# Packing V into 16-bit parts: the element operations go from VectorE to GpSimd, in two-operand instructions

## The chip, the cores and the metric

The kernel runs on one core of a Trainium2 chip. The metric is device time in microseconds for one execution. Before the change it is 1028.72 us, the median of three runs (1028.23 to 1029.83).

## What is computed

The reference mixes two branches over the same x (2048 rows of 512), with a gate of its own for each row:

```
g = sigmoid((x * gate_w).sum(-1))
q = x @ wq          # 32 heads of 16
k = x @ wk          # one head of 16, shared by all
v = x @ wv
a = softmax(q k^T / 4) v, heads joined, @ wo
b = silu(x @ w1) @ w2        # 512 -> 1792 -> 512
out = g * a + (1 - g) * b
```

All inputs and the output are fp32. The kernel keeps nearly fp32 exactness by splitting operands into two fp16 parts and adding three products, and, for the softmax's values, by "packing" V.

## The kernel before, in words

**Attention.** There are 16 rounds, one for each pair of a chunk of 512 query rows (c) and a group of 8 heads (o). A round has 32 steps; a step takes 64 keys. A step has two score units on TensorE (`scores`, L1186: 8 matmuls into a PSUM tile S), two exponentials on ScalarE (`exponential`, L1192, 128x1024 each, into a P buffer) and the product with V (`pv`, L1223). That product is made in one of two ways:

- in fp32 with V itself (the tile VF), whole (called W here) or in two halves of 256 columns (h);
- with the packed V (the tile VP, fp16): first a pass over the upper 16 bits of P (called A), then a pass over the remainder (called B). The remainder L = P - upper(P) is made by VectorE in two instructions of 128x1024 (`low`, L1198; its buffers are the L tiles, later the two raw tiles and freed parts of xs).

`decide` (L1400) lets a step take the packed way only if V's rows for that step are already packed: `k >= packed[0]` means W or h. Besides, VectorE must have room for the two remainders (`low_next`, L1411). So until the packing of the first 16 steps' keys is done, all steps take the fp32 way.

**The packing.** `v_parts` (L372) packs one half of V (16 of the 32 blocks of 64 keys) in five parts, all on VectorE: a maximum and a power of two per block (`first`), rounding to a high part `hi` and a rest `lo` (`first`, `second`), a sum of rest terms (`second`), then a chain of digit roundings (`third`, `fourth`), and two instructions that write VP (`fifth`). Its wide instructions have 128x256 elements, its small ones 128x16. The scratch tiles are U and T2 (T in the profile). `pack` (L1297) and `pack_next` hand the ten parts one after the other to VectorE's list of tasks.

**Other work.** TensorE also runs the feed-forward and the projections as a stream of passes (`Stream`, L1053; line 832; called F here), 8 matmuls to a pass when two outputs run side by side. Weights arrive in pieces: `Pieces.load` (L172) issues a DMA into one of two raw tiles, VectorE splits it in two instructions (L207, L208), and then the next DMA into that tile is issued **from GpSimd's queue** (L190). The cast of the hidden layer is also a DMA from GpSimd's queue (H<-e, L898). Otherwise GpSimd is idle after the start.

**The order.** Inside `attention` the order on every engine is written by a small planner: it holds a time for TensorE, ScalarE and VectorE (`now`), takes the engine whose next piece of work is ready first (`advance`, L1604) and emits it. Work for VectorE is put on a list by `task(due, ready, length, f)`, and the earliest due that is ready goes next (`dve_next`, L1539). Engines then run their instructions strictly in the order emitted, and wait on semaphores. The planner keeps no time for GpSimd.

Of the kernel before, what the change touches and what calls it, by code (L numbers as in the profile page):

```python
# [31 lines left out]
CAST, LEAD, ENDS = 3.0, 3, 2  # L32

# [20 lines left out]
def kernel(  # L54
# [317 lines left out]
    def v_parts(tiles, half):  # L372
# [5 lines left out]
        u, m, h, w = (ab[:, :, n:n + 1] for n in range(4))  # L378
        to = lambda t: t.to_broadcast([128, NKT, 16])
        nu, inv = (nus[:, n:n + 1].to_broadcast([128, NKT, 16]) for n in (0, 2))  # L380
        tt = lambda out, a, b, op: nc.vector.tensor_tensor(out, a, b, op=op)
        ts = lambda out, a, k: nc.vector.tensor_scalar(out, a, k, None, op0=OP.mult)
        stt = lambda out, a, k, b: nc.vector.scalar_tensor_tensor(out, a, k, b, op0=OP.mult, op1=OP.add)

        def first():
# [3 lines left out]
            ts(u, u, 2.0 ** -10)  # L389
# [3 lines left out]
            tt(hi, hi, to(m), OP.add)  # L393

        def second():
            tt(hi, hi, to(m), OP.subtract)
            tt(lo, V, hi, OP.subtract)
            tt(s, lo, nu, OP.mult)
            nc.vector.tensor_reduce(w, s, axis=AX.X, op=OP.add)

        def third():
            for a in MAGIC * 4.0 ** -DIG, -MAGIC * 4.0 ** -DIG, 0.5 * 4.0 ** -DIG:
                stt(w, u, a, w)
            tt(un, to(u), nu, OP.mult)
            stt(s, un, -0.5, to(w))
            stt(s, un, MAGIC, s)

        def fourth():
            stt(s, un, -MAGIC, s)
            tt(k[:, :, 1:15], s[:, :, 1:15], s[:, :, 0:14], OP.subtract)  # L410
            tt(k[:, :, 0:1], s[:, :, 0:1], s[:, :, 15:16], OP.subtract)
            nc.vector.tensor_copy(k[:, :, 15:16], s[:, :, 15:16])
            tt(k, k, inv, OP.mult)

        def fifth():
            tt(VP[:, these, 1:17], hi, k, OP.add)
            tt(VP[:, these, 17:32], lo[:, :, 0:15], k[:, :, 0:15], OP.subtract)

        return first, second, third, fourth, fifth


# [369 lines left out]
    def attention(ctx, scale_of, t_scale, shifts, split_pieces, chores, q_todo, early, gates_):  # L791
# [437 lines left out]
        def begin():  # L1229
# [22 lines left out]
            for a in range(2):  # L1252
# [7 lines left out]
                def copies(t, a=a, v4=v4):  # L1260
# [7 lines left out]
                    else:  # L1268
# [3 lines left out]
                        pack_next(pack(), t)  # L1272
# [24 lines left out]
        def pack():  # L1297
            t2 = wp.tile([128, 32, 32], F32, name="T2").rearrange("p a b -> p (a b)")
            tiles = [wp.tile([128, 512], F32, name="U"), t2[:, 0:512], t2[:, 512:1024]]
            for half in range(2):  # L1300
                for n, f in enumerate(v_parts(tiles, half)):
                    yield 1.7, f, (half + (n == 4)) * NKT

        def pack_next(gen, t):
            x = next(gen, None)
            if x:
                length, f, upto = x

                def run(t):
                    f()  # L1310
                    packed[0] = upto
                    pack_next(gen, t)

                task(t + 4, t, length, run)
# [74 lines left out]
        n_early, n_begin = [3 * KD * len(early)], [0]  # L1389
        packed, n_mm, n_exp, head = [0], [0], [0], [0]  # L1390
# [214 lines left out]

# [94 lines left out]
```

## Time and profile before

| | |
|---|---|
| median of three runs | 1028.72 us |
| span of the profiled execution | 1033.2 us |
| PE (TensorE) busy | 1012.3 us, 98% |
| ACT (ScalarE) busy | 993.1 us, 96% |
| DVE (VectorE) busy | 916.4 us, 89% |
| POOL (GpSimd) busy | 62.7 us, 6% |
| first exponential starts | 28.23 us |
| last TensorE instruction starts | 1024.22 us |

The profiled execution is known by its span; it lies 4.5 us above the median of the runs. Rows of a timeline give start, duration, engine, line, operation, output tile, input tiles and the number of instructions merged. Rows of groups give the count, the busy time in us and the mean in ns of one, and then the idle time of the engine before them. A busy PE is modelled, so a unit of TensorE work is priced here by the distance of its start from the next unit's start.

### The profile page before, as it was taken

Reading aid. Unit: us, or ns where it says so; the run is one execution under the profiler, and the core shown is the slowest. Engines: PE = TensorE matmul, PEld = TensorE weight load, DVE = VectorE, ACT = ScalarE, POOL = GpSimd, SP = SyncE. Lnnn points to the kernel's source line nnn. Section 1 sums busy time; section 2 is a strip of 40 time slices with the busy share of each in tenths; the row PEclk is TensorE's granted clock in tenths of the full one; section 3 lists DMA queues with packets and bytes.
Section 4 is the critical chain, followed back from the end, with each engine's and each line's share of the span. In section 5 each row is a group of like instructions: output and inputs, shape, how many; then the busy total and the mean of one; then the engine's idle time right before and its main releaser. Section 6 shows DMA issues by size and latency. Waiting matters only on the chain.

```text
span 1033.2 us, 69440 instructions
## 1 busy us (share of the span) xinstructions
PE 1012.3 (98%) x32605; PEld 615.0 (60%) x32605; DVE 916.4 (89%) x1191; ACT 993.1 (96%) x1109; POOL 62.7 (6%) x141
## 2 busy tenths in 40 slices
PE   8999999999999999999999999999999999999996
PEld 7345655565656666656566665566665565565563
DVE  7778887889899999999989899798999889989994
ACT  5899999999999999999999999999999999999994
POOL 5001111100000000000000000000000000000000
PEclk9999999999999999999999999999999999999999
DMA  5122322221011111100101110110111110100001
GB/s 207 53 76 65 93 58 61 70 62 19 15 19 41 39 36 30 20 20 15 35 16 35 50 30 20 30 25 10 34 32 25 33 48 10 35 10 14 10 4 47
DMA packets 28114, 40.12 MB, mean 39 GB/s; under 512 B 5689, under 2 KB 19370, under 8 KB 27818
## 3 DMA queue, kind: packets, MB, share of 16 engines
q0 software_dynamic: 10656, 15.73, 7.3%
q1 hardware_dynamic: 16442, 19.27, 5.9%
q8 instruction: 257, 4.21, 1.7%
q10 hardware_dynamic: 720, 0.59, 0.2%
q14 instruction: 39, 0.32, 0.1%
HBM read 19.98 MB, written 8.25 MB: 27 GB/s over the span
## 4 chain that ended last, share of the span: by engine, by line
PE 71%; issue 19%; ACT 6%; DVE 1%; DMA 1%; POOL 1%; SPq 0%; ACTq 0%; POOLq 0%; DVEq 0%
PE pm L832 26%; PE pv L1223 24%; PE S L1186 17%; ACT P L1192 4%; ACT xs L1192 1%; PE pm L836 1%; DMA xn<-in_A_x_dram 1%; PE pt L336 1%; POOL H L898 1%; PE pv L1211 1%; DMA H<-e 0%; ACT e L886 0%; DVE L L1198 0%; PE S L1179 0%; DVE e L889 0%
## 5 line engine op out<-in xcount | busy, mean ns | idle before, releaser
L1192 ACT ACTIVATE P<-S 128x1024 f32<-128x1024 f32 x764 | 731.4, 1081 | 11.8 <-PE S L1186 7.8
L1186 PE MATMUL S<-qb,KT 50*32 50x512 f16 x8096 | 471.6, 379 | 3.3 <-ACT P L1192 1.7
L1186 PEld LDWEIGHTS <-KT 50*32 50x32 f16 x8096 | 203.3, 90 | 186.6 <-issue 96.7
L1198 DVE TENSOR_TENSOR L<-P 128x1024 f16<-128x1024 f32 x242 | 288.8, 1216 | 20.0 <-ACT P L1192 16.7
L832 PE MATMUL pm<-xs,w1s 64*32 64x512 f16 x5376 | 274.9, 375 | 2.4 <-DVE e L889 1.7
L832 PE MATMUL pm<-w2s,H 64*32 64x512 f16 x5376 | 267.9, 375 | 2.0 <-DVE e L889 1.2
L1192 ACT ACTIVATE xs<-S 128x1024 f32<-128x1024 f32 x260 | 256.8, 1082 | 2.5 <-PE pv L1223 1.1
L1223 PE MATMUL pv<-P,VF 64*32 64x256 f32 (+1 forms) x4880 | 250.6, 450 | 0.3 <-issue 0.3
L832 PEld LDWEIGHTS <-w1s 64*32 64x32 f16 x5376 | 124.7, 92 | 49.8 <-issue 10.8
L832 PEld LDWEIGHTS <-H 64*32 64x32 f16 x5376 | 120.1, 93 | 44.3 <-issue 5.7
L1198 DVE TENSOR_TENSOR raw<-P 128x1024 f16<-128x1024 f32 x104 | 124.8, 1217 | 7.4 <-ACT P L1192 7.1
L1223 PEld LDWEIGHTS pv<-P,VF 64*32 64x32 f32 x4880 | 103.2, 106 | 32.6 <-issue 3.2
L1223 PEld LDWEIGHTS <-VP 64*32 64x32 f16 x3856 | 75.8, 92 | 34.3 <-issue 5.3
L1198 DVE TENSOR_TENSOR L<-xs 128x1024 f16<-128x1024 f32 x72 | 86.5, 1217 | 4.8 <-ACT xs L1192 4.5
L1223 PE MATMUL pv<-L,VP 64*32 64x512 f16 x1256 | 90.6, 375 | 0.0
L832 PE MATMUL pm<-xs,wqs 64*32 64x512 f16 x1152 | 87.0, 375 | 0.0
L1223 PE MATMUL pv<-P,VP 64*32 64x512 bf16 x1384 | 82.7, 387 | 0.0
L1198 DVE TENSOR_TENSOR raw<-xs 128x1024 f16<-128x1024 f32 x64 | 76.9, 1216 | 5.8 <-ACT xs L1192 5.5
L1223 PE MATMUL pv<-xs,VF 64*32 64x256 f32 (+1 forms) x1584 | 76.5, 416 | 0.1
L898 POOL DMA_DIRECT2D H<-e x56 | 30.1, 537 | 733.7 <-DVE e L889 723.2
L832 PE MATMUL pm<-wo_s,O 64*32 64x512 f16 x1440 | 70.4, 375 | 0.1
L1223 PE MATMUL pv<-raw,VP 64*32 64x512 f16 x672 | 54.8, 375 | 0.0
(216 smaller groups left out, 724.1 us busy)
## 6 DMA issues: line engine op xcount, KB each, us to landing
H<-e POOLq DMA_DIRECT2D x56, 128.0 KB, 2.5
raw<-in_B_w_dram POOLq DMA_DIRECT2D x24, 256.0 KB, 3.0
qb<-qd SPq DMA_DIRECT2D x180, 32.0 KB
xn<-in_A_x_dram SPq DMA_DIRECT2D x8, 512.0 KB
out_dram<-acc SPq DMA_DIRECT2D x14, 256.0 KB
qd<-qx SPq DMA_DIRECT2D x13, 256.0 KB
raw<-in_A_wo_dram POOLq DMA_DIRECT2D x4, 256.0 KB, 2.9
qb<-sh SPq DMA_DIRECT2D x60, 2.0 KB
```

The source lines that it names most:

```text
L336: nc.tensor.transpose(pt[:, kt], xn[c].rearrange("p t (d k) -> p t k d", k=KD)[:, t, kt], ident)
L832: nc.tensor.matmul(self.bank[32 * m:32 * m + 32], l(i, rows, 32 * m), r(j, rows), start=first, stop=last)
L836: nc.tensor.matmul(self.bank, l(i, slice(0, 128), 0, 128), r(j, slice(0, 128)), start=first, stop=last)
L898: nc.gpsimd.dma_start(H[:, 0], e)
L1186: nc.tensor.matmul(sc[32 * m:32 * m + 32, f], KT[b:b + 50, k0:k0 + 32], qtile[i][b:b + 50, m // 2, j], start=True, stop=True)
L1192: nc.scalar.activation(probs[s][:, 2 * j:2 * j + 2], banks.pop(p), AF.Exp, scale=scale_of(*rounds[steps[s][0]]))
L1198: nc.vector.tensor_tensor(lows[s, j], probs[s][:, js], upper(probs[s])[:, js], op=OP.subtract)
L1211: nc.tensor.matmul(pvs[i][h][32 * j:32 * j + 32, 256 * q:256 * q + 256], VF[r, NK - 2 * PAIRS + 2 * u + a], probs[s][r, j, 256 * a:256 * a ...
L1223: nc.tensor.matmul(pvs[i][h][32 * j:32 * j + 32, q], a[r], b[r, q], start=k == 0 and n != "B", stop=k == NK - 1 and n in "BMW")
```

## The change

`v_parts` now has six parts. The maximum, the three small instructions after it (`first`) and the sum over the rest terms stay on VectorE; all other instructions are issued on GpSimd. GpSimd gets no three-operand form, so each `scalar_tensor_tensor` becomes a `tensor_scalar` and a `tensor_tensor`. `pack` no longer goes through VectorE's list but for `first` and the sum: it emits a GpSimd part when the planner's three clocks have all passed its time, takes a length for it from the table VPACK, and lets the steps use VP when that length is over.

```
+VPACK = 0.0, 2.4, 1.6, 3.2, 3.8, 2.0
...
-        tt = lambda out, a, b, op: nc.vector.tensor_tensor(out, a, b, op=op)
-        ts = lambda out, a, k: nc.vector.tensor_scalar(out, a, k, None, op0=OP.mult)
-        stt = lambda out, a, k, b: nc.vector.scalar_tensor_tensor(out, a, k, b, op0=OP.mult, op1=OP.add)
+        tt = lambda out, a, b, op: nc.gpsimd.tensor_tensor(out, a, b, op=op)
+        ts = lambda out, a, k: nc.gpsimd.tensor_scalar(out, a, k, None, op0=OP.mult)
...
             nc.vector.tensor_scalar(u.bitcast(U32), u.bitcast(U32), 0x7F800000, None, op0=OP.bitwise_and)
-            ts(u, u, 2.0 ** -10)
+            nc.vector.tensor_scalar(u, u, 2.0 ** -10, None, op0=OP.mult)
+
+        def second():
             ts(h, u, 0.5)
             ts(m, u, MAGIC)
             tt(hi, V, to(h), OP.subtract)
             tt(hi, hi, to(m), OP.add)
-
-        def second():
             tt(hi, hi, to(m), OP.subtract)
+
+        def third():
             tt(lo, V, hi, OP.subtract)
             tt(s, lo, nu, OP.mult)
-            nc.vector.tensor_reduce(w, s, axis=AX.X, op=OP.add)
-
-        def third():
+            return lambda: nc.vector.tensor_reduce(w, s, axis=AX.X, op=OP.add)
+
+        def fourth():
             for a in MAGIC * 4.0 ** -DIG, -MAGIC * 4.0 ** -DIG, 0.5 * 4.0 ** -DIG:
-                stt(w, u, a, w)
+                ts(n1, u, a)
+                tt(w, n1, w, OP.add)
             tt(un, to(u), nu, OP.mult)
-            stt(s, un, -0.5, to(w))
-            stt(s, un, MAGIC, s)
-
-        def fourth():
-            stt(s, un, -MAGIC, s)
+            ts(s, un, 0.5)
+            tt(s, to(w), s, OP.subtract)
+
+        def fifth():
+            ts(k, un, MAGIC)
+            tt(s, s, k, OP.add)
+            tt(s, s, k, OP.subtract)
             tt(k[:, :, 1:15], s[:, :, 1:15], s[:, :, 0:14], OP.subtract)
             tt(k[:, :, 0:1], s[:, :, 0:1], s[:, :, 15:16], OP.subtract)
-            nc.vector.tensor_copy(k[:, :, 15:16], s[:, :, 15:16])
+            nc.gpsimd.tensor_copy(k[:, :, 15:16], s[:, :, 15:16])
+
+        def sixth():
             tt(k, k, inv, OP.mult)
-
-        def fifth():
             tt(VP[:, these, 1:17], hi, k, OP.add)
             tt(VP[:, these, 17:32], lo[:, :, 0:15], k[:, :, 0:15], OP.subtract)
...
+            def follow(t):
+                if not todo:
+                    return
+                half, n, f = todo.pop(0)
+                if n == 0:
+                    task(t + 1, t, 1.2, lambda t: (f(), follow(t)))
+                    return
+                rest = f()
+                t += VPACK[n]
+                if rest:
+                    task(t, t, 0.5, lambda t: reduced(t, rest))
+                    return
+                packed_at.append((t, (half + (n == 5)) * NKT))
+                follow_at.append((t, follow))
...
         def advance():
 
+            while follow_at and follow_at[0][0] <= min(now.values()):
+                t, f = follow_at.pop(0)
+                f(t)
+            while packed_at and packed_at[0][0] <= min(now.values()):
+                packed[0] = max(packed[0], packed_at.pop(0)[1])
```

The packing takes part in the planner's times, so the order of the whole program after it changes. Line numbers rise by one from L33 on and by six behind `v_parts`: L207 and L208 become L208 and L209, L1198 becomes L1204. Three places matter below.

On GpSimd, the queue in the middle of round 0 before the change holds only DMA issues. `raw` are the two weight buffers, `in_A_wq` and `in_B_w` the weights in memory, H<-e a cast:

```order
L190 DMA raw_81<-in_B_w_dram 128x512
L190 DMA raw_82<-in_B_w_dram 128x512
L190 DMA raw_81<-in_A_wq_dram 128x2x256
L190 DMA raw_82<-in_A_wq_dram 128x2x256
L190 DMA raw_81<-in_B_w_dram 128x512
L898 DMA H<-e 128x512
```

The same place after the change (the end of `fourth`, then `fifth` and `sixth` of V's second half):

```order
L382 TENSOR_TENSOR T_842<-T_842 128x256
L383 TENSOR_SCALAR T_842<-T_842 128x256
L382 TENSOR_TENSOR T_842<-T_842 128x256 x2
L382 TENSOR_TENSOR T_842<-T_842 128x16x14
L382 TENSOR_TENSOR T_842<-T_842 128x16
L418 COPY T_842<-T_842 128x16
L191 DMA raw_82<-in_A_wq_dram 128x2x256
L191 DMA raw_81<-in_B_w_dram 128x512
L382 TENSOR_TENSOR T_842<-T_842,nus 128x256
L382 TENSOR_TENSOR VP<-U,T_842 128x16x16
L382 TENSOR_TENSOR VP<-U,T_842 128x16x15
```

The second wq piece's DMA now stands behind `fourth` and `fifth` in one queue, and `sixth`, which writes VP, stands behind two DMA issues, each of which waits for VectorE to be done with its raw buffer.

On VectorE, before the change, around the first remainders (L<-P) of round 0 and the second half's packing:

```order
L962 TENSOR_SCALAR O<-pm 128x512
L963 SCALAR_TENSOR_TENSOR O<-pm,O 128x512
L1198 TENSOR_TENSOR L<-P 128x1024
L207 TENSOR_SCALAR w1s<-raw_81 128x512
L208 SCALAR_TENSOR_TENSOR w1s<-raw_82,w1s 128x512
L974 TENSOR_SCALAR O<-O 128x512
L381 TENSOR_TENSOR U<-U,T_842 128x256
L381 TENSOR_TENSOR U<-VF,U 128x256
L381 TENSOR_TENSOR T_842<-U,nus 128x256
L399 TENSOR_REDUCE T_842<-T_842 128x16
L1198 TENSOR_TENSOR L<-P 128x1024
```

And after it:

```order
L968 TENSOR_SCALAR O<-pm 128x512
L969 SCALAR_TENSOR_TENSOR O<-pm,O 128x512
L980 TENSOR_SCALAR O<-O 128x512
L1204 TENSOR_TENSOR L<-P 128x1024
L208 TENSOR_SCALAR w1s<-raw_82 128x512
L209 SCALAR_TENSOR_TENSOR w1s<-raw_81,w1s 128x512
L402 TENSOR_REDUCE T_842<-T_842 128x16
L1204 TENSOR_TENSOR L<-P 128x1024
```

The three wide packing instructions are gone, but the sum (L402) stays between a step's two remainders, and it now waits for GpSimd.

At the end of the program VectorE's rows before the change are these, for the last half of the last round (pv to T to U to O, then the output rows acc):

```order
L1112 STREAM_TRANSPOSE T_33779<-pv_32086 128x256
L1112 STREAM_TRANSPOSE T_33779<-pv_32087 128x256
L1116 TENSOR_TENSOR T_33779<-T_33779 128x16x15
L1119 TENSOR_TENSOR U<-T_33779,nus 128x112
L1123 TENSOR_REDUCE T_33779<-U 128x16
L1125 RECIPROCAL rr<-T_33779 128x16
L1127 TENSOR_TENSOR U<-T_33779,rr 128x2x8x16
L1136 STREAM_TRANSPOSE O<-U 128x256
```

After the change the last of these rows are:

```order
L1131 RECIPROCAL rr<-T_33705 128x16
L1133 TENSOR_TENSOR U<-T_33705,rr 128x2x8x16
L819 SCALAR_TENSOR_TENSOR acc<-pm,g_65,acc 128x512 x2
L1142 STREAM_TRANSPOSE O<-U 128x256
L819 SCALAR_TENSOR_TENSOR acc<-S,g_119,acc 128x512 x2
```

Two additions of feed-forward outputs (acc<-pm) now stand ahead of the last transposition.

29 lines of the change are left out of this document (12 added, 17 removed).

## The prediction, as put on record

> **What bounds the kernel now.** I read the page first: busy shares, then the chain of work that ended last.
>
> ```profile
> span 1033.2 us, 69440 instructions
> PE 1012.3 (98%) x32605; PEld 615.0 (60%) x32605; DVE 916.4 (89%) x1191; ACT 993.1 (96%) x1109; POOL 62.7 (6%) x141
> PE 71%; issue 19%; ACT 6%; DVE 1%; DMA 1%; POOL 1%; SPq 0%; ACTq 0%; POOLq 0%; DVEq 0%
> ```
>
> TensorE carries the chain (71%, and most of "issue" is its own order), ScalarE follows closely. VectorE, which the change relieves, has 1% of it. So time on VectorE counts only as it lets TensorE do less, or as TensorE waits for it.
>
> TensorE's work is counted in units whose price is the distance between starts. This timeline of TensorE is at the step where the second half of V is first used packed:
>
> ```profile
> 80.38 1.09 PE L1223 MATMUL pv<-P,VF 64*32 64x512 f32 x16
> 81.24 0.45 PE L1186 MATMUL S<-qb,KT 50*32 50x512 f16 x8
> ...
> 82.19 0.42 PE L1223 MATMUL pv<-P,VP 64*32 64x512 bf16 x8
> 82.42 0.41 PE L1223 MATMUL pv<-L,VP 64*32 64x512 f16 x8
> 82.64 0.62 PE L832 MATMUL pm<-xs,w1s 64*32 64x512 f16 x16
> 83.07 0.41 PE L1186 MATMUL S<-qb,KT 50*32 50x512 f16 x8
> 83.29 0.43 PE L1223 MATMUL pv<-P,VP 64*32 64x512 bf16 x8
> 83.53 0.62 PE L1223 MATMUL pv<-P,VF 64*32 64x256 f32 x16
> 83.96 0.41 PE L1186 MATMUL S<-qb,KT 50*32 50x512 f16 x8
> ```
>
> W (fp32, 512 columns) costs 0.86, h (256 columns) 0.43, A 0.23, B 0.22, a score unit 0.22, two F passes 0.43. A packed step costs TensorE 0.45 against 0.86, and VectorE two remainders:
>
> ```profile
> L1198 DVE TENSOR_TENSOR L<-P 128x1024 f16<-128x1024 f32 x242 | 288.8, 1216 | 20.0 <-ACT P L1192 16.7 <-PE pv L1223 2.0 <-issue 0.3
> 28.23 1.94 ACT L1192 ACTIVATE P<-S 128x1024 f32<-128x1024 f32 x2 [0.32 <-PE S L1186]
> 1021.19 1.98 PE L1650 MATMUL S<-qx,O 128*128 128x512 f32 x4
> ```
>
> From the first exponential to the last projection are 993 us. The units of the order before (1036 score units, 126 W, 290 h, 241 A, 241 B, 1707 F passes, 62 early products) sum to 954 us by these prices, so TensorE waits about 39 us in all, some 2.4 us in each of 16 rounds.
>
> **Part 1, TensorE's work.** Counting the two orders row by row, the change has A +2, B +2, W +1, h -6, F passes +6 (six fewer with two outputs side by side, twelve more with one output alone). That is 0.46 + 0.44 + 0.86 - 2.58 + 1.29 = **+0.5 us**. Of it, eight F passes (1.7 us) stand behind the very last half product in the new order, none in the old: ahead of that point TensorE has 1.3 us less to do.
>
> **Part 2, the end.** Old timeline:
>
> ```profile
> 1021.26 0.78 DVE L1112 STREAM_TRANSPOSE T<-pv 128x256 f32<-128x256 f32 x2
> 1023.63 0.45 DVE L1136 STREAM_TRANSPOSE O<-U 128x256 f32<-128x256 f32 x1
> 1024.22 1.96 PE L1650 MATMUL pv<-qx,O 128*128 128x512 f32 x4 [1.05 <-DVE O L1136]
> 1020.43 0.75 DVE L813 SCALAR_TENSOR_TENSOR acc<-pm,g,acc 128x512 f32<-128x512 f32 x1 [2.24 <-PE pm L832]
> ```
>
> From the last product the chain of normalisation takes 2.4 us to L1136, and the last projection follows at 3.0 while the first projection (2.0) is hidden. In the new order the eight passes (1.7) come before the first projection, and two additions of 0.75 each before L1142: 2.4 + 1.5 + 0.45 gives 4.3, so the last projection starts at about 4.4: **+1.4 us**. With the 1.3 saved ahead of it, parts 1 and 2 give +0.1 if TensorE sets the pace up to there, and +1.4 if ScalarE does, since its exponentials are the same in number. Both are nearly full (98% and 96%); I take the middle, **+0.7 us** for parts 1 and 2.
>
> **Part 3, VectorE.** The packing's lines on VectorE, in the window 38 to 84 us, for L381, L383, L382 and L412 in this order:
>
> ```profile
> 38.00:84.00 46.00, 8.37 (x22) 1.00 0.24 74
> 38.00:84.00 46.00, 3.62 (x12) 1.00 0.24 74
> 38.00:84.00 46.00, 0.89 (x6) 1.00 0.24 74
> 38.00:84.00 46.00, 0.35 (x2) 1.00 0.24 74
> ```
>
> Of these 13.2 us two small ones (0.3) stay; 12.9 go. Four more remainders come back (4 x 1.216 = 4.9), so VectorE has 8.0 us less. I value this at zero beyond the two packed steps of part 1: it is freed in round 0, before or while V is packed, when a step may not use it. Its bounds: 0 if later rounds are as before; -3.4 if all 8.0 became packed steps (3.3 of them, 0.41 each) and their F passes ran earlier.
>
> **Part 4, GpSimd's chain.** What GpSimd costs is bounded by its only arithmetic in the trace, and by its small copies and its DMA issues:
>
> ```profile
> L491 POOL TENSOR_SCALAR wqr<-wqr 128x512 f32<-128x512 f32 x2 | 3.0, 1492 | 5.6 <-ACT wqs L490 5.5
> L492 POOL TENSOR_TENSOR wqs<-wqr,wqs 128x512 f16<-128x512 f32 x2 | 2.3, 1166 | 0.2
> L329 POOL COPY wkv<-gwr 128x4 f32<-128x4 f32 x1 | 0.2, 193 | 0.2 <-DMA gwr<-in_gate_w_dram 0.2
> 74.17 0.73 POOL L190 DMA_DIRECT2D raw<-in_A_wq_dram  x1 [4.83 <-DVE w1s L208]
> raw<-in_A_wq_dram POOLq DMA_DIRECT2D x2, 256.0 KB, 3.4
> raw<-in_B_w_dram POOLq DMA_DIRECT2D x24, 256.0 KB, 3.0
> ```
>
> With 0.19 as the fixed part, 256 elements take 0.68 (two tensors) or 0.84 (one); the ends are 0.19 and the whole 1.17 or 1.49. Between one instruction and a dependent one 0.08 is added. Per half there are 13 wide two-tensor instructions, 2 wide and 5 small with one tensor, 4 small with two and a copy: 12.4 + 25 x 0.08 = 14.4 us. By part: second 2.8, third 1.5, fourth 4.1, fifth 3.7, sixth 2.2.
>
> ```profile
> 38.30 0.41 DVE L147 TENSOR_REDUCE T<-VF 128x16 f32<-128x256 f32 x1
> 63.88 0.42 PE L1223 MATMUL pv<-P,VP 64*32 64x512 bf16 x8
> 46.15 21.67 ACT L1192 ACTIVATE P<-S 128x1024 f32<-128x1024 f32 x21 [0.73 <-PE S L1186]
> ```
>
> First half: `first` starts at 38.3 and ends at 39.4. With the sum (0.6 with its two hand-overs) and a DMA issue (0.55) before `third` and before `fifth`, `fifth` ends at 39.4 + 2.8 + 0.55 + 1.5 + 0.6 + 4.1 + 0.55 + 3.7 = 53.2; one more DMA and `sixth` write VP by 56. The first packed use is step 15 in the new order (step 13 before, at 63.88), 3.9 us of units later: 67.8. It is covered by 11 us.
>
> Second half: the piece whose DMA stands behind `fifth` of the first half lands at 53.2 + 0.55 + 3.0 = 56.8, VectorE splits it (1.1), `first` (1.1) ends at 59.0, `third` at 63.3. Step 15's first exponential is the 31st; the ACT row holds the 16th to the 36th, 1.03 apart, so it ends at 62.6. Then come the first remainder (63.8), a piece (64.9), the sum L402 (65.3) and the second remainder (66.6); B of step 15 is due at 68.2: 1.6 us of cover, and 1.6 more for GpSimd. `fourth` and `fifth` end at 73.1; only now is the second wq piece's DMA issued (0.73, landing 3.4: 77.2), and VectorE's queue holds that piece (78.3), with a bound's two instructions (1.35) and the two remainders of step 23 (82.1) behind it. GpSimd issues the next DMA and writes VP by 81.2. By the units between, A of step 23 is due 15.6 after A of step 15, at 83.4, and B at 83.9: about 2 us of cover. So at the middle price nothing stalls, but the covers are thin, the second because a DMA issue is caught in the packing.
>
> What eats the cover is that GpSimd and VectorE hinder each other. Before, at the start:
>
> ```profile
> 3.55 2.10 DVE L265 TENSOR_SCALAR hj<-hj,pm 128x32 f32<-128x32 f32 x1
> 3.78 0.94 POOL L224 MEMSET VP<- 128x1024 f16 x1
> 4.67 0.94 POOL L224 MEMSET VF<- 128x1024 f32 x1
> 5.69 0.32 DVE L266 TENSOR_SCALAR hm<-hj 128x32 f32<-128x32 f32 x1
> 14.94 1.49 POOL L491 TENSOR_SCALAR wqr<-wqr 128x512 f32<-128x512 f32 x1
> 15.24 0.59 DVE L129 SCALAR_TENSOR_TENSOR wo_s<-wkv,wo_s 128x256 f16<-128x256 f32 x1
> L208 DVE SCALAR_TENSOR_TENSOR w1s<-raw,w1s 128x256 f16<-128x256 f32 x4 | 1.7, 416 | 0.0
> ```
>
> L265 needed 2.10 where L266, of the same size, took 0.32; it ended as GpSimd's memset of VF did (5.61). L129 with two inputs in SBUF ran inside L491 and took 0.59 against 0.416 of its shape elsewhere: 0.17 more, not a full stop. In the 24 us up to L402 VectorE has 6.2 us of such work (four pieces, two magnitudes, a remainder). If it holds GpSimd up for half of that, `third` slips by 3.1 to 66.4, L402 ends 1.5 late and the second remainder at 68.1, just on time. In the second stretch about 4 us of pieces and remainders add 2: 3.5 against a cover of 1.8 to 2.2, so step 23 loses 1.3 to 1.7. I take **+1.6 us**. Lower end 0 (cover holds). Upper end: all 26 wide two-tensor instructions at the whole 1.17, that is 0.49 more each; the second remainder of step 15 then ends at 72.3 (4.1 late) and VP is written at 91.0 (another 3.5 late): +7.6. TensorE takes its units in order, so a stall shifts all behind it.
>
> The Trainium skill, "SBUF — State Buffer", section "Who interferes with whom", has a stricter rule, and it speaks against this change: VectorE in a two-port mode, or with two SBUF inputs against a GpSimd instruction that reads, excludes GpSimd for the whole instruction, and the reverse. L265 agrees with it; L129, which did not wait for the end of L491, does not as the trace draws it. By the rule every one of those VectorE instructions stops the chain for its full length; the second rival below is what that comes to here.
>
> **Sum.** +0.7 + 1.6 = **+2.3 us**: a span of 1035.5 against 1033.2. On the median of the runs, 1028.72, that is 1031.0.
>
> **Rivals.**
>
> *Covered (0.33).* The stalls don't come, and the 0.7 of parts 1 and 2 stays: 1029.4. For it: the middle price leaves 1.6 and 2 us at the two places, 11 in the first half. Against it: the two rows of hindrance.
>
> *Full exclusion (0.09).* GpSimd waits out all 6.2 us of VectorE's contending work before L402 (`third` at 69.5, the second remainder at 71.2: step 15 loses 3.0). L402 is 4.6 late, 4 us follow, and of these 8.6 the cover of 1.8 and the 3.0 already lost go off: step 23 loses 3.8. With the 0.7 that is +7.5, 1036.2. It decides as soon as half of it, 3.1 us of holding up, is passed. For it stands L265, against it L129.
>
> *Waits drawn anew (faster, 0.20).* The order is new in all 16 rounds, and its 39 us of waits are not the same ones. A tenth less is 3.9 us, and VectorE's 8.0 us, if moved into later rounds, would make just such waits on remainders shorter: 1028.7 + 0.1 - 3.9 = 1024.9 (0.1, since then TensorE sets the pace). The same lot can fall the other way; that is in the forecast's range. It decides if the stalls of part 4 stay under 1.7 us, so that 2.1 of the gain is left. Against it: VectorE has 1% of the chain.
>
> *The change doesn't do what it says:* VectorE is freed of 12.9 us, but the order gives it only four more remainders. That is in all the cases above, as the zero of part 3.
>
> **Chances.** Forecast +2.3 (own range 1030.8 to 1034) 0.38; full exclusion 0.09; covered 0.33; faster 0.20. About 0.2%, 2.1 us, is what a measurement of this kernel can tell from no change. Faster 0.20, within 0.33, slower 0.47. The range, 1025.3 to 1036.0, leaves out half of the fast case and most of full exclusion, 0.18 together; the upper bound of part 4 (0.7 + 7.6, 1037.0) is the same case and lies outside too.
>
> **What would show it.** Right: wide GpSimd instructions at 0.6 to 0.9 us; L402 waiting for GpSimd; a TensorE pause before B of step 15 or A of step 23 of 1 to 2 us; a wq DMA issued right behind `fifth`; the last projection 4.4 us after the last product. Wrong: no pause there and a span under 1033; or wide instructions beyond 1.2 us, with pauses of over 4 us; or a difference that arises in rounds 1 to 15, in waits that have no counterpart in the packing.

## The result, and the profile after

The changed kernel takes 1037.3 us (median of 6 runs, 1034.65 to 1038.36) against 1029.28 us for the kernel before in the same series (6 runs, 1027.45 to 1030.45): a ratio of 1.0073, 95% interval 1.0059 to 1.0087, or 8.0 us **slower**. I had forecast 1031.0 with an upper end of 1036.0: the right sign, less than a third of the size.

The two profiled executions don't show this difference in their spans, since the one of before, at 1033.2 us, was longer than any timed run of before, and the one of after was its fastest. So the traces are compared by places, and sizes are taken from timed runs. First the page of the changed kernel, its span, busy times and the shares of the chain that ended last:

```profile
span 1032.9 us, 69350 instructions
...
PE 1010.0 (98%) x32557; PEld 606.9 (59%) x32557; DVE 912.3 (88%) x1155; ACT 991.1 (96%) x1109; POOL 93.8 (9%) x191
...
PE 49%; issue 28%; ACT 12%; DVE 5%; POOL 3%; DMA 3%; SPq 0%; ACTq 0%; POOLq 0%; DVEq 0%
```

VectorE lost 4.1 us of work and GpSimd gained 31; GpSimd, which had 1% of the chain, now has 3%, VectorE 5% instead of 1%. So a little of the two engines' work has come onto the path. Where, the waits of TensorE between 60 and 95 us say (what waited, for whom, us in total, times, longest); it is the only row of that answer:

```profile
PE pm L838 <- DVE O L997: 1.7, 1, 1.7
```

Now the same place by engine. GpSimd's timeline of the changed kernel, the second half of V (start, duration, engine, line; in brackets the idle time before and what ended it):

```profile
71.48 0.88 POOL L383 TENSOR_SCALAR T<-T 128x256 f32<-128x256 f32 x1
72.44 2.38 POOL L382 TENSOR_TENSOR T<-T 128x256 f32<-128x256 f32 x4
74.77 0.21 POOL L418 COPY T<-T 128x16 f32<-128x16 f32 x1
74.92 0.77 POOL L191 DMA_DIRECT2D raw<-in_A_wq_dram  x1
79.56 0.57 POOL L191 DMA_DIRECT2D raw<-in_B_w_dram  x1 [3.87 <-DVE wqs L209]
80.15 0.74 POOL L382 TENSOR_TENSOR T<-T,nus 128x256 f32<-128x256 f32 x1
80.97 3.25 POOL L382 TENSOR_TENSOR VP<-U,T 128x256 f16<-128x256 f32 x2
```

And VectorE's beside it:

```profile
78.23 0.43 DVE L208 TENSOR_SCALAR wqs<-raw 128x512 f16<-128x512 f32 x1 [5.99 <-DMA raw<-in_A_wq_dram]
78.58 0.68 DVE L209 SCALAR_TENSOR_TENSOR wqs<-raw,wqs 128x512 f16<-128x512 f32 x1
79.18 0.68 DVE L997 TENSOR_SCALAR O<-pm 64x512 f16<-64x512 f32 x1
79.89 0.68 DVE L440 TENSOR_REDUCE um<-O 64x1 f32<-64x512 f16 x1
80.49 3.16 DVE L1204 TENSOR_TENSOR L<-P 128x1024 f16<-128x1024 f32 x2
```

These rows are a **knot of three queues**. The load of the second wq piece stands behind `fifth` (the copy L418 is its last instruction) and is issued at 74.92. VectorE stands idle for 5.99 us with that piece at the head of its queue; behind the piece stands L997, one of the bound's two instructions, which empties a bank of PSUM (the memory that TensorE writes), and TensorE pauses for that bank. GpSimd's next load then waits 3.87 us for VectorE to free a piece's buffer (L209), and behind that load stand the last three packing instructions.

At the end of the program VectorE has these rows, to be held against those of before in the prediction:

```profile
1020.51 0.78 DVE L1118 STREAM_TRANSPOSE T<-pv 128x256 f32<-128x256 f32 x2 [2.43 <-PE pv L1217]
...
1022.76 1.40 DVE L819 SCALAR_TENSOR_TENSOR acc<-pm,g,acc 128x512 f32<-128x512 f32 x2
1024.08 0.43 DVE L1142 STREAM_TRANSPOSE O<-U 128x256 f32<-128x256 f32 x1
```

And TensorE's last projections, the second of them held back until L1142:

```profile
1022.40 1.99 PE L1669 MATMUL S<-qx,O 128*128 128x512 f32 x4
1024.66 1.96 PE L1669 MATMUL pv<-qx,O 128*128 128x512 f32 x4 [0.27 <-DVE O L1142]
```

From the start of L1118 to that of the last projection are 4.15 us; before, from L1112 to L1650, 2.96.

### The profile page after: what moved, and what is told of

It reads as the page before. It is cut to its first block, busy times and chain, and to the rows that moved or that the text cites. A ratio compares the mean times of both kernels' runs of the same rounds, so it can differ in the third digit from the quotient of the medians.

```text
span 1032.9 us, 69350 instructions
## 1 busy us (share of the span) xinstructions
PE 1010.0 (98%) x32557; PEld 606.9 (59%) x32557; DVE 912.3 (88%) x1155; ACT 991.1 (96%) x1109; POOL 93.8 (9%) x191
## 4 chain that ended last, share of the span: by engine, by line
PE 49%; issue 28%; ACT 12%; DVE 5%; POOL 3%; DMA 3%; SPq 0%; ACTq 0%; POOLq 0%; DVEq 0%
PE pm L838 19%; PE pv L1229 16%; PE S L1192 12%; ACT P L1198 8%; ACT xs L1198 3%; DVE L L1204 1%; DMA xn<-in_A_x_dram 1%; ACT e L892 1%; POOL T L382 1%; DMA H<-e 1%; POOL H L904 1%; DVE e L895 1%; DVE raw L1204 1%; POOL T L383 1%; PE pv L1217 1%
## 5 line engine op out<-in xcount | busy, mean ns | idle before, releaser
L1198 ACT ACTIVATE P<-S 128x1024 f32<-128x1024 f32 x768 | 736.4, 1088 | 12.2 <-PE S L1192 6.4
L1192 PE MATMUL S<-qb,KT 50*32 50x512 f16 x8096 | 450.7, 380 | 5.1 <-ACT xs L1198 2.6
L1204 DVE TENSOR_TENSOR L<-P 128x1024 f16<-128x1024 f32 x234 | 279.9, 1220 | 18.5 <-ACT P L1198 17.6
L838 PE MATMUL pm<-w2s,H 64*32 64x512 f16 x5376 | 274.2, 375 | 2.2 <-DVE e L895 1.1
L838 PE MATMUL pm<-xs,w1s 64*32 64x512 f16 x5376 | 268.6, 375 | 2.9 <-DVE O L997 1.7
L1198 ACT ACTIVATE xs<-S 128x1024 f32<-128x1024 f32 x256 | 256.2, 1096 | 3.0 <-PE pv L1229 1.6
L838 PEld LDWEIGHTS <-w1s 64*32 64x32 f16 x5376 | 119.6, 93 | 45.7 <-issue 8.2
L1204 DVE TENSOR_TENSOR raw<-P 128x1024 f16<-128x1024 f32 x112 | 134.3, 1215 | 4.1 <-ACT P L1198 3.6
L1204 DVE TENSOR_TENSOR L<-xs 128x1024 f16<-128x1024 f32 x82 | 98.6, 1217 | 7.0 <-ACT xs L1198 6.9
L1204 DVE TENSOR_TENSOR raw<-xs 128x1024 f16<-128x1024 f32 x58 | 69.8, 1215 | 1.9 <-ACT xs L1198 1.7
L838 PE MATMUL pm<-wo_s,O 64*32 64x512 f16 x1440 | 69.7, 375 | 0.0
L1229 PE MATMUL pv<-xs,VF 64*32 64x256 f32 (+1 forms) x1392 | 68.8, 437 | 0.0
```

What stands on the lines that cost most here:

```text
L838: nc.tensor.matmul(self.bank[32 * m:32 * m + 32], l(i, rows, 32 * m), r(j, rows), start=first, stop=last)
L1192: nc.tensor.matmul(sc[32 * m:32 * m + 32, f], KT[b:b + 50, k0:k0 + 32], qtile[i][b:b + 50, m // 2, j], start=True, stop=True)
L1198: nc.scalar.activation(probs[s][:, 2 * j:2 * j + 2], banks.pop(p), AF.Exp, scale=scale_of(*rounds[steps[s][0]]))
L1204: nc.vector.tensor_tensor(lows[s, j], probs[s][:, js], upper(probs[s])[:, js], op=OP.subtract)
L1229: nc.tensor.matmul(pvs[i][h][32 * j:32 * j + 32, q], a[r], b[r, q], start=k == 0 and n != "B", stop=k == NK - 1 and n in "BMW")
```

## The experiments

They ran on other chips, where both kernels take some 7 to 13 us longer and the runs of the kernel before spread over 8 to 15 us; each ratio is to runs of the kernel before on the same chip, in turn with it. Two theories at first: the pauses that GpSimd causes in round 0 (S, later K for the knot), against an order of the later rounds that happens to be worse (O, then R, later L for the lottery). As a third, H: VectorE and GpSimd slow each other whatever the queues do. A fourth, Z, concerns one run alone: that it was quick because VP held zeros.

Three lengths were read from each trace: round 0 (from the first exponential's start to the 65th's), rounds 1 to 15 (to the end of the last exponential), and the end (from there to the last instruction). All us, one execution each; "end" in the second column names the form of the end, of before or of the change:

| run | order, end | packing | round 0 | rounds 1-15 | end | ratio, 95% |
|---|---|---|---|---|---|---|
| before (first profile) | before | VectorE | 67.6 | 924.3 | 13.1 | 1 |
| e1_before_again | before | VectorE | 67.6 | 927.8 | 12.9 | 1.0012 (0.9989-1.0035) |
| e4_old_order | before | GpSimd | 68.8 | 937.7 | 12.3 | 1.0015 (0.9991-1.0038) |
| after (first profile) | change | GpSimd | 69.2 | 921.6 | 14.2 | 1.0073 (1.0059-1.0087) |
| e5_after_again | change | GpSimd | 71.1 | 931.3 | 15.0 | 1.0068 (1.0045-1.0091) |
| e15_after_third | change | GpSimd | 71.0 | 933.2 | 14.6 | 1.0046 (1.0026-1.0065) |
| e2_no_pack | change | none | 67.2 | 934.9 | 15.3 | 1.0018 (0.9995-1.0041) |
| e6_copy_pack | change | copies | 67.2 | 928.0 | 14.6 | 1.0028 (1.0007-1.0049) |
| e16_copy_again | change | copies | 67.2 | 930.0 | 14.6 | 1.0042 (1.0017-1.0067) |
| e14_first_half | change | half on GpSimd | 67.2 | 931.9 | 15.1 | 1.0021 (1.0003-1.0040) |
| e17_one_load_sp | change | GpSimd | 67.2 | 933.0 | 15.0 | 1.0022 (1.0002-1.0043) |
| e3_loads_sp | change | GpSimd | 69.7 | 934.6 | 15.0 | 1.0077 (1.0052-1.0102) |
| e13_loads_act4 | change | GpSimd | 69.5 | 928.3 | 14.7 | 1.0047 (1.0024-1.0070) |
| e7_slow_prices | other, change | GpSimd | 70.9 | 928.6 | 13.7 | 1.0032 (1.0008-1.0055) |
| e11_sp_slow | other, change | GpSimd | 69.5 | 935.6 | 14.4 | 1.0084 (1.0055-1.0113) |
| e12_other_end | other, near before | GpSimd | 69.7 | 937.9 | 13.5 | 1.0111 (1.0078-1.0143) |
| e8_redraw | other, change | VectorE | 68.2 | 932.6 | 14.2 | 1.0045 (1.0024-1.0065) |
| e9_redraw8 | other, before | VectorE | 68.0 | 927.3 | 12.4 | 1.0027 (1.0006-1.0049) |
| e10_redraw2 | other, change | VectorE | 67.0 | 935.4 | 14.7 | 1.0088 (1.0057-1.0119) |

Rounds 1 to 15 vary by over 10 us between traces of one order (921.6 to 933.2 in the changed kernel), so there single traces decide nothing. Round 0 is another matter: measured from the first exponential's start, the first 48 exponentials of after, e5_after_again, e15_after_third, e6_copy_pack and e17_one_load_sp start within 0.05 us of each other. There 0.1 us counts.

**Order and packing apart.** The kernel before, once more:

> The kernel before, unchanged, for a second profile of it. The profiled execution of before spanned 1033.2 us, more than its timed runs took as a whole (1027.45 to 1030.45), so its waits may not be those of a usual run. Every theory expects a ratio of 1.000 within 0.1%. If the first profile was an unusual execution, this one should span some 1026 to 1029 us, and the 4 us less should be found in rounds 13 and 14, where the first one waited 4.1 and 5.2 us against about 2.4 in the other rounds. If it spans 1033 again, a profiled execution of this kernel is simply longer than a timed one and the two profiles may be compared as they are.

Its ratio is 1.0012, with an interval of 0.9989 to 1.0035: differences of about 0.002 can't be told from nothing here. Its span, 1036.1 us, comes from a chip on which all runs are longer, so it doesn't say whether the first profile was unusual; its round 0 is that of the first to 0.01 us. Then the changed order without GpSimd's packing:

```
-        tt = lambda out, a, b, op: nc.gpsimd.tensor_tensor(out, a, b, op=op)
-        ts = lambda out, a, k: nc.gpsimd.tensor_scalar(out, a, k, None, op0=OP.mult)
+        tt = lambda out, a, b, op: None
+        ts = lambda out, a, k: None
...
-            return lambda: nc.vector.tensor_reduce(w, s, axis=AX.X, op=OP.add)
+            return lambda: nc.vector.tensor_reduce(w, V, axis=AX.X, op=OP.add)
...
-            nc.gpsimd.tensor_copy(k[:, :, 15:16], s[:, :, 15:16])
```

> The changed kernel, with the order on TensorE, ScalarE and VectorE as it is, but none of the packing's instructions on GpSimd; the sum on VectorE reads V itself, so it waits for nothing. VP stays zero, so this leaves out the packing. Theory S (GpSimd's packing stalls the program in round 0: a DMA issue caught behind it, VectorE held up at the sum and by shared access): the loss of 8.0 us goes, time 1029 to 1031 (ratio about 1.000 to 1.002). Theory O (the new order of all rounds and the longer tail cost it, whatever GpSimd does): time stays at 1035 to 1038 (ratio 1.006 to 1.009). A split, as the changed kernel's profile of round 0 suggests (one pause of 2.1 us at 77.8 us): 2 us less, 1035.3.

1.0018, with round 0 at 67.2 and no wait of TensorE's listed between 60 and 100 us. The order before with the packing on GpSimd:

```
...
-        tt = lambda out, a, b, op: nc.vector.tensor_tensor(out, a, b, op=op)
+        tt = lambda out, a, b, op: nc.gpsimd.tensor_tensor(out, a, b, op=op)
...
```

> The kernel before with its own order and its five parts, but with the packing's element instructions on GpSimd as in the change; the maximum, the small ones and the sum stay on VectorE, the sum one part later so that VectorE does not wait long for it. So GpSimd does the same work with the old order of TensorE, ScalarE and the rest of VectorE. Theory S: it is as slow as the change or slower, since the old plan takes the packing as done earlier: 1035 to 1040. Theory O: the new order being the cause, this one stays at 1028 to 1031, with at most a pause of 1 to 2 us in round 0.

1.0015: here TensorE waits twice, 1.0 us in sum, for remainders, and round 0 is 1.3 us longer. In neither run alone are the 8 us to be found.

**The loads off GpSimd.** The edit, and what was expected of it:

```
-                self.load(nc.gpsimd)
+                self.load(nc.sync)
```

> The changed kernel, with the weight pieces' DMAs issued from SyncE's queue and not from GpSimd's, the other engines' order unchanged. GpSimd's packing stays. Theory S in the form of the prediction (the second wq piece's DMA is caught behind fifth, and VectorE idles 6.0 us for it): TensorE's pause of 2.1 us at 77.8 us goes and with it 2 to 3 us of the time: 1034.5 to 1035.5. Theory O: within 1 us of the changed kernel, 1036.5 to 1038, since the pause is given back by waits that come anyway. If SyncE's queue delays the pieces more than GpSimd's did, the time rises, and SyncE's DMA rows show it.

1.0077: no help. The pause at 78 us is gone, but two others, of 1.4 and 0.7 us, have come at 87 and 89; TensorE waits for a remainder (L1204) in both. SP's queue in this run (DMA issues; q tiles are `qb`) shows why:

```profile
72.13 0.38 SPq L191 DMA_DIRECT2D raw<-in_A_wq_dram  x1
72.73 0.64 SPq L438 DMA_DIRECT2D sh<-e  x2
73.41 0.32 SPq L279 DMA_DIRECT2D qb<-qd  x1
...
82.15 0.42 SPq L281 DMA_DIRECT2D qb<-qd  x1
82.62 0.54 SPq L283 DMA_DIRECT2D qb<-sh  x1
83.27 0.37 SPq L191 DMA_DIRECT2D raw<-in_B_w_dram  x1
```

The wq piece leaves at 72.13, but the next piece stands behind the q tiles' transfers until 83.27, and on VectorE two remainders stand behind that piece:

```profile
85.93 0.43 DVE L208 TENSOR_SCALAR w2s<-raw 128x512 f16<-128x512 f32 x1 [4.21 <-DMA raw<-in_B_w_dram]
86.27 0.68 DVE L209 SCALAR_TENSOR_TENSOR wqs<-raw,wqs 128x512 f16<-128x512 f32 x1
86.88 2.35 DVE L1204 TENSOR_TENSOR L<-P 128x1024 f16<-128x1024 f32 x2
```

The blocking had only changed its queue.

**The yardsticks.** The changed kernel and the changed order with copies, each on two more chips:

> The changed kernel unaltered, as the yardstick for the runs beside it. Both theories expect the ratio found first, 1.0073 (1.006 to 1.009), with round 0 about 69.2 us long (before: 67.6) and the stretch after the last exponential 14 us (before: 13.1). If the extra time were a matter of one chip alone, the ratio here would come out near 1.003, the sum of what the run without packing (1.0018) and the run with the old order (1.0015) showed.

> The changed order, but V is only copied into VP (two GpSimd copies per half; the splitting into 16-bit parts is left out), so VP holds ordinary values and not the zeros that it held in the run without packing. Theory S (GpSimd's 14 us per half and what it does to VectorE cost the time): like the run without packing, a ratio of 1.001 to 1.004, round 0 at 67.2 or less. Theory Z (the run without packing was quick because it multiplied by zeros): like the changed kernel, 1.006 to 1.009. Theory R (the new order of rounds 1 to 15 costs the time, whatever packs V): also 1.006 to 1.009.

```
...
+            nc.gpsimd.tensor_copy(VP[:, these, 1:17], V)
+            nc.gpsimd.tensor_copy(VP[:, these, 17:32], V[:, :, 0:15])
```

> The changed kernel unaltered, the upper end of the scale: 1.007 (1.0045 to 1.009 in the runs before).

> The changed order with V only copied into VP (its splitting is left out), the lower end of the scale: 1.0023 (1.0018 and 1.0028 in the runs before), so that the packing on GpSimd is worth 0.0045 to 0.005. If the difference to the changed kernel beside it is under 0.002, most of the loss belongs to the order and not to GpSimd.

1.0068 against 1.0028, then 1.0046 against 1.0042. The second pair came out well under the one expectation (1.007) and above the other (1.0023), and its difference, under 0.002, speaks by the rule set beforehand for the order and not for GpSimd. The two pairs don't agree, so the ratios alone decide nothing. With ordinary values in VP round 0 is as long as with the zeros (67.17 and 67.16), so nothing is left that theory Z would have to explain there. Round 0, where traces agree to hundredths, is 71.1 and 71.0 against 67.2 and 67.2.

Why does the knot cost 1.9 us in the first trace of the changed kernel and 3.7 to 3.9 in the other two? In all three TensorE pauses for L997; after the pause it is quick in the first (rows of TensorE, then the row of a stretch, with the granted clock third from the end):

```profile
79.91 0.41 PE L838 MATMUL pm<-xs,w1s 64*32 64x512 f16 x8 [1.71 <-DVE O L997]
80.34 1.27 PE L838 MATMUL pm<-xs,w1s 64*32 64x512 f16 x40
79.91:83.32 3.41, 3.41 (x112) 1.93 (x119) 3.41 (x3) 2.33 (x3) 3.31 (x4) 1.00 0.43 112
```

And it is slow in e5_after_again:

```profile
80.53 0.63 PE L838 MATMUL pm<-xs,w1s 64*32 64x512 f16 x8 [2.16 <-DVE O L997]
81.33 2.38 PE L838 MATMUL pm<-xs,w1s 64*32 64x512 f16 x40
80.34:83.75 3.41, 3.22 (x64) 1.53 (x71) 3.38 (x4) 1.03 (x1) 3.31 (x4) 0.50 0.42 105
```

The granted clock is 0.50 for 3.41 us, which takes 1.7 us of TensorE's work away; in e15_after_third the same follows a pause of 1.9 us, from 80.84 on. So in these two traces the pause is only about half of what the knot costs.

**Which half.**

```
-        tt = lambda out, a, b, op: nc.gpsimd.tensor_tensor(out, a, b, op=op)
+        tt = lambda out, a, b, op: half or nc.gpsimd.tensor_tensor(out, a, b, op=op)
...
```

> The changed order; the first half of V is packed on GpSimd as in the change, the second half only copied (its splitting is left out). Theory K: nothing of the loss is in the first half, so the run is like the one with copies only (round 0 at 67.2, the ratio equal within 0.001). Theory H: half of the loss is in the first half, so the run stands midway, 0.002 above the one with copies.

Round 0 is 67.2, as K expects. The ratio, 1.0021, is 0.0021 under that of the copies beside it, which neither theory expects and which is within the noise. In round 0 the first half costs nothing; all that GpSimd costs there comes in the second.

**Untying the knot.** First by way of ScalarE:

```
+            if w is wq or w is w2 and g == 0 and a < 1:
+                queue = nc.scalar
```

> The changed kernel; the loads of three weight pieces (the two wq pieces and the first w2 piece) are issued by ScalarE, where nothing of the packing and no q tile's transfer stands before them. Theory K (the knot of the queues in the second half): the 2.1 to 2.5 us pause of TensorE at 78 us is gone, VP's second half is written by 77 and not at 84 us, round 0 is 67.2 to 68 us, and the ratio is 0.002 to 0.003 below that of the changed kernel beside it. Theory H (VectorE and GpSimd slow each other, whatever the queues do): pauses of the same sum turn up elsewhere in round 0, and the ratio stays.

The pause at 78 us is gone and VP is written by 78.7 (K expects 77), yet round 0 stays at 69.5 and the ratio at 1.0047, as H expects. ScalarE's timeline of this run decides it:

```profile
61.92 2.98 ACT L1200 ACTIVATE P<-S 128x1024 f32<-128x1024 f32 x3
66.32 0.39 ACTq L193 DMA_DIRECT2D raw<-in_A_wq_dram  x1
66.81 3.77 ACT L1200 ACTIVATE P<-S 128x1024 f32<-128x1024 f32 x4 [1.91 <-DVE w1s L211]
```

The load waited in ScalarE's queue for VectorE to free the buffer, and the exponentials behind it 1.91 us with it: an in-order queue once more. So the last run moves one load only, the one that is caught:

```
+            if w is wq and a == 1:
+                queue = nc.sync
```

> The changed kernel with one edit: the load of the second wq piece, which is caught behind the packing's fifth part, is issued by SP; all others stay on GpSimd. With the loads all on SP that piece was issued at 72 us without harm. Theory K: VectorE has the piece by 75 to 76 us and not 78 to 79, the pause of TensorE at 78 us is gone, VP's second half is written by 80 us, round 0 falls from 69.2 to 71.1 to 67.2 to 67.6, and the ratio to that of the order alone, 1.0015 to 1.004. Theory H (GpSimd's and VectorE's mutual hindrance): round 0 stays over 69 and the ratio at 1.0045 to 1.007.

All the packing is on GpSimd, with its right values in VP, and round 0 is 67.2; from the 49th exponential on, where the changed kernel loses 1.9 to 3.9 us within three exponentials, this run follows the one with copies to 0.01 us until the round's end. The ratio is 1.0022, measured on a chip on which the changed kernel did not run beside it. GpSimd's rows of this run, whose first exponential starts 0.6 us later than the changed kernel's:

```profile
75.91 0.21 POOL L420 COPY T<-T 128x16 f32<-128x16 f32 x1
76.14 0.60 POOL L193 DMA_DIRECT2D raw<-in_B_w_dram  x1
76.77 0.74 POOL L384 TENSOR_TENSOR T<-T,nus 128x256 f32<-128x256 f32 x1
77.59 1.40 POOL L384 TENSOR_TENSOR VP<-U,T 128x256 f16<-128x256 f32 x2
```

And VectorE's:

```profile
74.45 0.43 DVE L210 TENSOR_SCALAR wqs<-raw 128x512 f16<-128x512 f32 x1 [1.62 <-DMA raw<-in_A_wq_dram]
74.80 1.05 DVE L211 SCALAR_TENSOR_TENSOR wqs<-raw,wqs 128x512 f16<-128x512 f32 x1
77.75 0.68 DVE L999 TENSOR_SCALAR O<-pm 64x512 f16<-64x512 f32 x1 [1.90 <-PE pm L435]
...
79.07 2.34 DVE L1206 TENSOR_TENSOR L<-P 128x1024 f16<-128x1024 f32 x2
```

VP is written by 78.98, not 84.22, and the bound's instruction (L999 here, L997 in the changed kernel) now waits for TensorE, at 77.75. Theory K is shown for round 0, and H is out there as a cost on the path.

**The plan's prices.** GpSimd's measured durations in the plan:

```
-VPACK = 0.0, 2.4, 1.6, 3.2, 3.8, 2.0
+VPACK = 0.0, 3.6, 2.4, 5.2, 5.5, 4.5
```

> The changed kernel, planned with the durations that its own trace shows for GpSimd's parts (3.6, 2.4, 5.2, 5.5, 4.5 us in place of 2.4, 1.6, 3.2, 3.8, 2.0). The first remainders' products then come later and the long form of the product is used ten times more in round 0. Theory S: the 2.1 us pause of TensorE at 78 us is gone, round 0 is 0.8 us (the added units) above 67.2 to 67.6, and the ratio falls to 1.002 to 1.005. Theory R: the order is drawn anew once more, so the ratio may fall anywhere from 0.999 to 1.010, and need not go with the pause.

The ratio, 1.0032, is as S expected, but not by its mechanism: the pause at 78 us is gone and round 0 is 70.9 all the same. A knot of the same kind has come 17 us later, with another transfer. GpSimd's rows of this run:

```profile
90.13 2.39 POOL L382 TENSOR_TENSOR T<-T 128x256 f32<-128x256 f32 x4
92.46 0.21 POOL L418 COPY T<-T 128x16 f32<-128x16 f32 x1
92.61 0.59 POOL L904 DMA_DIRECT2D H<-e  x1
```

VectorE's:

```profile
88.24 0.68 DVE L895 SCALAR_TENSOR_TENSOR e<-e,pm 128x512 f32<-128x512 f32 x1
...
95.03 1.44 DVE L908 TENSOR_TENSOR H<-e,H 128x512 f16<-128x512 f32 x1 [0.73 <-DMA H<-e]
...
96.99 0.67 DVE L895 SCALAR_TENSOR_TENSOR e<-e,pm 128x512 f32<-128x512 f32 x1
```

And the longest of TensorE's waits there:

```profile
PE pm L838 <- DVE e L895: 1.8, 1, 1.8
```

H's transfer could go when L895 had ended, at 88.92, and goes behind `fifth` at 92.61; VectorE's L908 waits for it, and the next L895 stands behind that, with a bank that TensorE waits for.

Then this plan with all loads on SP, and a further one with an end nearer to that of before:

> The changed kernel with both cures at once: the loads of the weight pieces issued by SP, so that none is caught behind the packing, and the plan told GpSimd's measured durations, so that no product waits for VP. Theory S: both kinds of pause of round 0 are gone (none over 1.1 us between 70 and 100 us), round 0 is 68 us, and the ratio is 1.001 to 1.003, below the 1.0032 of the plan with measured durations alone. Rival: the cure was in the order of the later rounds, and the pauses of round 0 don't count; then the ratio stays at 1.003 or above although they are gone.

> As the run with both cures, with 3.8, 2.4, 5.4, 4.8, 3.6 for GpSimd's parts: the planner then comes to an end like that of before (78 F passes of four matmuls and not 90, fewer behind the last half-product). The end as a cost of its own: the stretch after the last exponential falls from 14.6 to about 13 us, and the ratio is 0.001 to 0.002 below that of the run with both cures. If the end is no cost, the two are equal; if the lot of the later rounds outweighs both, they differ by more than 0.003 either way.

Both missed: 1.0084 and 1.0111. SP's transfers hold pieces back in the rounds that follow; in the second run VectorE waits so at 206 us, with two remainders behind the piece, while TensorE pauses 3.6 us and then has 3.41 us at a granted clock of 0.50. The load left SP at 202.74, behind an unbroken run of such transfers since 192.71; VectorE's rows:

```profile
206.45 0.43 DVE L208 TENSOR_SCALAR w2s<-raw 128x512 f16<-128x512 f32 x1 [6.14 <-DMA raw<-in_B_w_dram]
...
207.40 2.35 DVE L1204 TENSOR_TENSOR L<-P 128x1024 f16<-128x1024 f32 x2
```

The first run, too, has such a slow stretch, with a pause of 2.9 us at 143 us. So neither run tells the value of the end.

**The order alone.** The kernel before with other spacings of the packing's parts in the plan (5, 8 and 2 in place of 4 us), no instruction moved to another engine:

```
-                task(t + 4, t, length, run)
+                task(t + 5, t, length, run)
```

> The kernel before, all packing on VectorE; only the planner's spacing of the packing's parts is 5 us and not 4, which draws the order of all rounds anew (its units of TensorE are 0.4 us fewer up to the last round, its end is that of the changed kernel, with the shorter F passes behind the last half-product). Theory S: a ratio of 1.000 to 1.002 (the end's 1.2 us less 0.4). Theory R: an order drawn anew is worth several us in either direction, a ratio outside 0.998 to 1.003.

> The kernel before, all packing on VectorE, with 8 us for the planner's spacing of the packing's parts in place of 4. TensorE's units end 0.8 us above those of before, and the end is that of before (no F pass more behind the last half-product). Theory L (an order drawn anew is a lottery, and the order of before is a good lot): 1.001 to 1.005, with a stretch after the last exponential near 12.9 us. Theory S (only the end and GpSimd's stalls cost time): 1.0008, inside 0.9995 to 1.002.

> The kernel before, all packing on VectorE, with 2 us for the spacing of the packing's parts in place of 4: TensorE's units come out equal to those of before (0.05 us more), the end is that of the changed kernel. Theory S: the end's 1.3 to 1.8 us alone, a ratio of 1.001 to 1.002. Theory L: like the order with 5 us, 1.003 to 1.006, or at random between 0.999 and 1.006.

1.0045, 1.0027 and 1.0088, none of them with a GpSimd instruction more. Theory S alone can't give these, and the last is beyond even what L expected (1.006). An order drawn anew costs 3 to 9 us here by itself, with up to 2.0 of it in the end. Its waits between 98 and 231 us in the slowest are many small ones, and I can't name one mechanism for them.

## Why the prediction was wrong, step by step

*The end (parts 1 and 2, taken +0.7).* Right in its rows behind the last product, without a term for what stands ahead of it. From its end to the last projection are 4.20 us in the trace of the change, 2.97 in that of before: +1.2 where I worked out +1.4. But the last product also ends 1.8 to 2.5 us after the last exponential in the ten traces with the changed order, 1.1 to 1.4 in the four with the end of before, on average 0.8 later. In the ten, 22 to 37 recorded matmuls of the feed-forward start between the two, in the four none or one. So TensorE still has work to do there when ScalarE is done. The ends average 14.8 us against 12.7: **+2.1**, not 0.7, over the bound of 1.4 that I had for "ScalarE paces". Whether the last exponential itself came earlier for the 1.3 us that TensorE was to save ahead of it, rounds 1 to 15 are too uneven to tell. No run takes the new end away from the changed order, so the 2.1 is read from rows and not tested.

*VectorE (part 3, taken zero).* Right as far as round 0 shows: with the knot untied it is 67.2 against 67.6, a gain of 0.4 in which the units' change is contained.

*GpSimd's chain (part 4, taken +1.6).* The prices held: the wide instructions took 0.65 to 0.81 mostly, the sum L402 waited 0.6 us for GpSimd twice, the first half was covered, the wq load went out right behind `fifth` at 74.92 (I had 73.1), and the piece was split by 79.3 (I had 78.3). **The step that failed** is the cover in "with a bound's two instructions (1.35) and the two remainders of step 23 (82.1) behind it": I named the instructions behind the piece, but asked of the remainders alone who waits for them. L997 reads a bank that TensorE needs next, and was due at 77.75 in the untied run, not at step 23's 83. Counted from the first exponential's start that is 49.26, and in the three traces of the changed kernel L997 starts at 51.28, 51.76 and 51.48, so 2.0 to 2.5 late. The exponentials lost 1.9, 3.9 and 3.7 us: **3.2** on average, twice my price. About 2 us of each loss is the pause; the rest, in the second and third trace, is TensorE at half its clock for 3.41 us behind the pause, a cost that the prediction has no term for.

The timed runs fit this, but only in their averages. The three ratios of the changed kernel average 1.0062, the five of its order without the knot (no packing, copies twice, half, one load moved) 1.0026: by that the knot is worth 0.0036 or 3.7 us. Each ratio has an interval of about 0.002 either way, and where both kinds ran on one chip the difference is 0.0040 on one, 0.0004 and 0.0025 on the other. If 3.7 is taken, what is left, 2.7 us, is the end's 2.1 and round 0's -0.4 but for 1.0. Of the 8.0 first measured, the end (2.1) and the knot (3.2) are placed in rows, less 0.4 for round 0; the 3.1 left would have to be in rounds 1 to 15, where traces of one order differ by more than that, and I cannot place them; that part of the cause stays open. It isn't the clock, as far as the first two profiles show: in rounds 1 to 15 it is granted at 1.00 in both. Of the 6.4 us that the three ratios average to, 1.0 (with 3.7 for the knot) to 1.5 (with 3.2) are left.

*Full exclusion (0.09, 1036.2)* named nearly the right time for a wrong reason: with the knot untied the whole packing costs round 0 nothing. Hindrance itself exists. Where VectorE's remainders and GpSimd's writing of VP run together (80.49 to 84.22, above), the pairs take 3.16 and 3.25 us; apart, in the run with one load moved, 2.34 and 1.40, in sum 3.74: just the 3.73 us that both took together. The Trainium skill, "SBUF — State Buffer", section "Who interferes with whom", has such pairs exclude each other, and there the trace agrees with it in the sum. But neither engine stood still for one whole instruction of the other: all four were drawn out (1.49 and 1.75 us against 1.2, 1.60 and 1.69 against 0.7), and with the loads in time they never met.

*Covered (0.33)* failed by the knot. *Waits drawn anew (0.20, faster)* had a real mechanism and the wrong sign. I had the lot fall either way with equal ease; three other orders with the packing on VectorE all came out slower, by 0.3 to 0.9%. Beside these three the order of before is a good lot, and the 39 us of waits that I read in its trace gave no sign of whether a lot is good. Why the later rounds of one order wait more than those of another stays open.

## What to carry to other kernels

When work moves to an engine that also issues loads, list for each load what stands ahead of it on that queue, and for each instruction behind the loaded piece who waits for it, not only for the one that the change is about. Moving a caught load is a cure only on a queue that is free at that moment; here SP and ScalarE handed the blocking on, and one load moved, alone, untied it. A pause of TensorE can cost more than its length: look at the granted clock behind it, in more than one trace. And where a planner sets the order, first draw it anew without the change: that spread (here 0.3 to 0.9%, all on one side) is the floor under any gain or loss one wants to credit to the change itself.

## What the runs showed of the hardware

Executions of one program on different chips were alike to 0.05 us for the first 48 exponentials, then drifted apart, mostly in jumps of 0.4 to 1.2 us at changing places; that is how runs of one order spread by 10 us, at granted clocks of 0.995 to 1.000 over a whole execution. Between the first and the last exponential of the nineteen traces TensorE has fourteen pauses of over 1 us; the four of 1.9, 2.2, 2.9 and 3.6 us each come with 3.41 us at a granted clock of 0.50, which begin 1.9 to 4.2 us after the pause does; the ten of 1.0 to 1.8 us come with none. GpSimd's writing of VP (256 elements from two fp32 tensors) took 0.7 us alone and 1.6 to 1.7 beside a two-input VectorE instruction, which itself went from 1.2 to as much as 1.75. In GpSimd's queue a DMA issue that waits for its buffer stopped the arithmetic behind it for 3.87 us.
